# Another written-out order of all engine queues, with changed planner costs, in an attention and spectral-mixing kernel

## The chip, the cores and the metric

The kernel runs on one core of a Trainium2 chip. Five engines of the core work side by side, each on its own queue of instructions: TensorE (PE in the profile; its weight loads are listed apart as PEld) does matrix products from SBUF into PSUM, VectorE (DVE) and ScalarE (ACT) do elementwise work and can read PSUM, GpSimd (POOL) does elementwise work on SBUF, and SyncE (SP) issues most transfers between device memory and SBUF. The metric is the device time of one execution in microseconds, the median of several runs.

## The reference

Two branches read the same x, of 2048 rows and 640 columns in bf16; a gate mixes their outputs row by row.

```python
x = A_x
g = _sigmoid((x * gate_w).sum(-1, keepdims=True))
a = _A_ref(x, A_wq, A_wk, A_wv, A_wo, A_beta)
b = _B_ref(x, B_w_r, B_w_i)
return g * a + (1 - g) * b
```

Branch A projects x to q, k and v with 32 heads of 20 columns, and takes the rows in four segments of 512, one after another. In each segment it does causal softmax attention; from the second on it also reads a memory that the earlier segments left (a product of phi(k) and v, and the sum of phi(k), where phi(t) is t + 1 above zero and exp(t) below). Both are mixed by a gate for each head, and the result is projected with wo:

```python
p = _softmax(logits, axis=-1)
a_dot = jnp.einsum('bhqk,bhkd->bhqd', p, vs)
pq = phi(qs)
num = jnp.einsum('bhld,bhde->bhle', pq, M)
den = jnp.einsum('bhld,bhd->bhl', pq, z)[..., None] + 1e-06
a_mem = num / den
o = g * a_mem + (1.0 - g) * a_dot
```

Branch B transforms all of x by a two-dimensional real Fourier transform, multiplies it by a table of weights, and transforms it back:

```python
X = jnp.fft.rfft2(x.astype(jnp.float32), axes=(-2, -1))
W = w_r + 1j * w_i
X = X * W
y = jnp.fft.irfft2(X, s=(S, D), axes=(-2, -1)).astype(jnp.bfloat16)
```

(The last two blocks are cut and written without the wrapping functions.)

## The kernel before

The program is recorded first as a list of 2353 small operations, in the class `Kern`, and laid out and emitted afterwards by the class `Sched`. An operation names the engines that can do it, what it reads and writes, and a cost for each engine. Many evictions of PSUM have two engines to choose from (`copy_alts`: ScalarE or VectorE), and so have some additions from SBUF to SBUF (`either`: VectorE or GpSimd).

What sets the order is `ORDER` (L556), a tuple of 2353 numbers written into the kernel. Half of a number, rounded down, is the operation; its last bit picks the engine. For each engine the order of its instructions is that of the tuple. `schedule` (L109) walks through the queues with the costs, and from the times that it works out it places the PSUM banks (four for the attention logits, four for everything else, L552), the semaphores of transfers, and the point up to which earlier transfers must have landed before a new one is issued (`WINDOW`, 1,600,000 bytes in flight). Tile positions of TensorE, called modes in the code, also follow from the order: 0 for the full array, 1 for four rows of tiles (the logits), 2 for four columns of tiles. `emit` (L239) then writes the instructions with their waits. Since all matmul helpers issue at L496 (mode 2 pieces) and L498, all PSUM copies at L507 (ScalarE) and L509 (VectorE), and all transfers at L526 (transposed) and L528, the profile tells them apart by their tiles.

The work, with the names that the code gives it:

- *Loads* (`ld_...`, `xT`): x comes twice, once plain into `xsb` in eight pieces for branch B, and once transposed into `xT` for each segment; weights and tables follow. The first transposed piece feeds the first projections (`projd`). Sixteen dummy matmuls on a zeroed tile (`warm`) run before.
- *Branch A*: `proj` makes q and k, evicted (`ev_proj`) and stored (`st_q`, `st_k`), then loaded again with heads padded to 32 partitions (`pad_q`, `pad_k`). `vproj` makes v. The logits are 80 units `qk` of four PSUM banks each; ScalarE's exp (L1137) empties each unit into `ex`, GpSimd zeroes the part above the diagonal (`mask`, L1140), `pv` multiplies with v, and VectorE scales the result into `on` (L1167, L1170, L1172). phi is an exp on ScalarE (L1010) and a max and a min on VectorE (L1021, L1022). The memory is updated (`mupd`, `m_add`, `m_mask`) and read (`memrd`, L1078 to L1082), and added by `addmem` (L1177). `on` is stored (`st_o`), loaded transposed (`oT`) and projected with wo (`oproj`, L496).
- *Branch B*: `fold` (L860, L865) adds and subtracts halves of x, and matmuls named F1, D, T, Tb, Db and Fb apply the transforms from tables. Their evictions are `ev_F1`, `ev_D`, `ev_Tb`, `ev_Db`; `W_mul` (L1287) and `W_add` (L1292) multiply by the weights; `sum_Db` (L1333) leaves the result in `G`.
- *Gate*: a few four-column operations for each segment (L937 to L955, of which L947 and L948 cast the gate to two bf16 halves), a transposing matmul (`gateT`), a store, and a load that spreads it over partitions (`gbc`). `gate_tab` (L968) multiplies it into a table by which Fb brings branch B into the PSUM bank of the output; `oproj` adds branch A there, `final` evicts it, and `st_out` and `st_part` store it.

The softmax here doesn't subtract the row's maximum and nothing guards it: scores larger than these inputs give would overflow.

## Time and profile before

| what | value |
|---|---|
| median of 4 runs | 246.53 us (246.17 to 247.04) |
| the profiled execution | 247.91 us |
| its span, first to last instruction | 246.2 us |
| mean granted TensorE clock | 0.993 |
| busy: TensorE, weight loads | 231.8, 140.2 us |
| busy: VectorE, ScalarE, GpSimd | 198.7, 201.5, 132.1 us |
| moved by DMA | 36.71 MB |

A busy time is the union of an engine's instructions, in microseconds. Matmuls are pipelined, so a TensorE that shows as busy need not be at its peak. In a row of an instruction the order is: start, length, engine, line, operation, output and inputs, shapes, and in brackets the idle time of the engine ahead of it with what ended it. A chain is followed back from the last instruction, at each step to what released it; its shares are shares of the span.

### The profile page before, as it was taken

The page shows a single profiled execution, that of the slowest core. Times are in us where ns is not written, and L with a number is a line of the kernel's source. Part 1 is how long each engine was busy: PE and PEld are TensorE (multiplying, and loading weights), DVE is VectorE, ACT ScalarE, POOL GpSimd, SP SyncE. Part 2 cuts the span into 40 slices and gives each one's busy share as a digit, 9 for nine tenths or more (in the row PEclk, how much of TensorE's full clock was granted, in tenths as well). Part 3 has the DMA queues.
Part 4 walks back from the last instruction along what each step waited for, and adds up shares of the span by engine and source line. Part 5 has one row for each costly group of instructions (what it writes and reads, how often), then busy time and mean ns, then how long its engine had stood idle before and what let it go on. Part 6 is the DMA issues. An engine that isn't in the chain of part 4 may idle for free.

```text
span 246.2 us, 8884 instructions
## 1 busy us (share of the span) xinstructions
PE 231.8 (94%) x3681; PEld 140.2 (57%) x3702; DVE 198.7 (81%) x534; ACT 201.5 (82%) x204; POOL 132.1 (54%) x200
## 2 busy tenths in 40 slices
PE   7899999999899999999888999999899999999994
PEld 2344565556556557556543565655555657667683
DVE  1489997988999898889997999989999975643743
ACT  2088799999998999999874998888899878798820
POOL 8421861262557684464974385646567656407610
PEclk9999999999999999999997999999999999999999
DMA  7998966695695666766442546313353857685224
GB/s 183 331 360 220 215 172 173 198 203 136 149 176 111 173 123 143 234 183 200 107 99 53 143 115 186 97 59 104 111 111 68 213 148 79 81 124 112 79 67 125
DMA packets 55880, 36.71 MB, mean 149 GB/s; under 512 B 31792, under 2 KB 52128, under 8 KB 55840
## 3 DMA queue, kind: packets, MB, share of 16 engines
q1 hardware_dynamic: 54144, 35.32, 58.3%
q10 hardware_dynamic: 1696, 0.82, 1.1%
q8 instruction: 29, 0.48, 0.8%
q14 instruction: 11, 0.09, 0.1%
HBM read 19.86 MB, written 9.71 MB: 120 GB/s over the span
## 4 chain that ended last, share of the span: by engine, by line
PE 65%; DVE 21%; DMA 6%; issue 3%; ACT 2%; SPq 1%; POOL 0%; DVEq 0%
PE psum L498 57%; PE psum L496 8%; DVE Pt L1287 5%; DMA xT<-in_A_x_dram 2%; DMA oT<-o_scr 2%; DMA o_scr<-on 2%; DVE qu L509 2%; DVE Cp L509 2%; ACT ex L1137 1%; SPq L528 1%; DVE Yt L1292 1%; DVE va L1045 1%; DVE on L1172 1%; DVE Ac L509 1%; DVE phk L1022 1%
## 5 line engine op out<-in xcount | busy, mean ns | idle before, releaser
L1137 ACT ACTIVATE ex<-psum 128x2048 bf16<-128x2048 f32 x80 | 150.2, 1878 | 17.9 <-PE psum L498 16.7
L1140 POOL TENSOR_SCALAR_AFFINE_SELECT ex<-ex 128x512 bf16<-128x512 bf16 x128 | 81.0, 653 | 72.7 <-ACT ex L1137 68.7
L498 PEld LDWEIGHTS psum<-va,ex 128*128 128x128 bf16 x1280 | 39.0, 96 | 5.8 <-issue 1.3
L498 PE MATMUL psum<-va,ex 128*128 128x21 bf16 x1280 | 41.2, 173 | 0.3 <-issue 0.2
L498 PE MATMUL psum<-qp,kp 20*128 20x384 bf16 (+3 forms) x512 | 31.7, 301 | 1.3 <-ACT ex L1137 0.3
L498 PE MATMUL psum<-wv,xT 128*128 128x500 bf16 (+1 forms) x160 | 32.0, 301 | 0.4 <-issue 0.2
L498 PE MATMUL psum<-xT,wk 128*128 128x512 bf16 (+1 forms) x129 | 30.5, 386 | 1.5 <-DMA xT<-in_A_x_dram 1.0
L498 PE MATMUL psum<-xT,wq 128*128 128x512 bf16 (+1 forms) x125 | 29.9, 388 | 1.4 <-DVE Bt L509 1.2
L1287 DVE TENSOR_TENSOR Pt<-psum,Wt 128x642 bf16<-128x642 f32 x32 | 25.4, 822 | 0.8 <-PE psum L498 0.5
L496 PE MATMUL psum<-wo,oT 128*32 128x320 bf16 x480 | 23.2, 300 | 0.3 <-issue 0.3
L498 PEld LDWEIGHTS psum<-qp,kp 20*128 20x128 bf16 x512 | 9.1, 92 | 18.4 <-ACT ex L1137 9.9
L509 DVE CAST ot<-psum 128x320 bf16<-128x320 f32 x21 | 10.0, 490 | 11.7 <-PE psum L496 8.6
L498 PE MATMUL psum<-big,Ac 128*128 128x321 bf16 (+2 forms) x96 | 17.9, 257 | 1.2 <-DVE Cp L509 0.4
L498 PEld LDWEIGHTS psum<-wv,xT 128*128 128x128 bf16 x160 | 13.3, 97 | 10.0 <-DVE Ac L509 0.8
L1045 DVE TENSOR_TENSOR va<-psum,ebx 128x500 bf16<-128x500 f32 (+1 forms) x32 | 15.2, 484 | 3.6 <-PE psum L498 2.8
L498 PE MATMUL psum<-tt,Yt 128*128 128x256 bf16 (+1 forms) x96 | 17.3, 277 | 0.5 <-DVE qu L509 0.2
L509 DVE CAST qu<-psum 128x512 bf16<-128x512 f32 x20 | 13.7, 687 | 4.8 <-PE psum L498 4.8
L1292 POOL TENSOR_TENSOR Yt<-Pt 128x321 bf16<-128x321 bf16 x18 | 13.4, 756 | 7.2 <-DVE Pt L1287 4.7
L498 PEld LDWEIGHTS psum<-xT,wk 128*128 128x128 bf16 (+1 forms) x140 | 10.1, 98 | 11.8 <-issue 3.8
L1333 DVE TENSOR_TENSOR G<-eo,psum 128x320 bf16<-128x320 f32 x32 | 14.9, 480 | 1.7 <-PE psum L496 0.9
L1177 POOL TENSOR_TENSOR on<-on,mem 128x320 bf16<-128x320 bf16 x16 | 12.8, 807 | 5.8 <-DVE on L1172 5.8
L1172 DVE TENSOR_TENSOR on<-psum,rs 128x320 bf16<-128x320 f32 x32 | 15.3, 481 | 0.6
(85 smaller groups left out, 379.7 us busy)
## 6 DMA issues: line engine op xcount, KB each, us to landing
tt<-tab_tt SPq DMA_DIRECT2D x16, 256.0 KB, 3.3
xsb<-in_A_x_dram SPq DMA_DIRECT2D x8, 320.0 KB
kp<-k_scr SPq DMA_DIRECT2D x28, 80.0 KB
qp<-q_scr SPq DMA_DIRECT2D x28, 80.0 KB
o_scr<-on SPq DMA_DIRECT2D x12, 160.0 KB
out_dram<-ot SPq DMA_DIRECT2D x12, 160.0 KB
q_scr<-qu SPq DMA_DIRECT2D x6, 256.0 KB
k_scr<-qu SPq DMA_DIRECT2D x6, 256.0 KB, 3.3
```

Of the source, the lines that this page charges most:

```text
L496: h = e.matmul(dst, wt, r_, start=st, stop=sp_, **{**kw, "tile_position": (0, q), "skip_group_check": True})
L498: h = e.matmul(o_, l_, r_, start=st, stop=sp_, **kw)
L509: alts["dve"] = (lambda e: e.tensor_copy(dst(), src()), 67 + 1.04 * n, 68.0)
L528: return e.dma_start(d_, s_)
L1045: self.one("dve", lambda e: e.tensor_tensor(va.ap(i * H * VW + h0 * VW, [VW, nh], [1, DH]), self.ps(bank, 0, [DH, nh], [1, DH]), self.ebx. ...
L1137: self.one("act", lambda e: e.activation(dst(), src(), ACT.Exp, scale=SC), 4 * width, [bank], [self.exb(s, g, j) for g, j in outs], prio - ...
L1140: self.one("pool", lambda e, g=g, j=j: e.affine_select(self.ex.ap(self.exo(s, g) + JOFF[j], [1280, 4], [1, P]), self.ex.ap(self.exo(s, g) ...
L1172: self.one("dve", lambda e, rs=rs, bank=bank, g=g: e.tensor_tensor(on.ap(80 * g, [D, 4], [DH, 4], [1, DH]), self.ps(bank, 0, [88, 4], [VW, ...
L1177: self.either(lambda e, g=g: e.tensor_tensor(on.ap(80 * g, [D, 4], [1, 80]), on.ap(80 * g, [D, 4], [1, 80]), self.mem.ap(80 * g, [D, 4], [ ...
L1287: self.one("dve", lambda e, ri=ri, Pt=Pt, Wt=Wt, bank=bank: e.tensor_tensor(Pt.ap(ri * 322, [644, 2], [1, KD]), self.ps(bank, 0, [0, 2], [ ...
L1292: fn = lambda e, r=r, a0=a0, a1=a1, op=op, Pt=Pt, Yt=Yt: e.tensor_tensor(Yt.ap(r * 322, [1, KD]), Pt.ap(a0 * 322, [1, KD]), Pt.ap(a1 * 322 ...
L1333: self.one("dve", lambda e, q=q, n2=n2, bank=bank, eo=eo: e.tensor_tensor(self.G.ap(n2 * D + 639 * q, [1 - 2 * q, 320]), eo.ap(q, [1, 320] ...
```

## The change

The tuple `ORDER` is replaced as a whole. With it come changed costs for the planning pass: higher fixed costs for GpSimd, other times for four kinds of transfer, the limit on transfers in flight counted when the pass picks the next instruction (before, it was only turned into a wait), and the two gate casts, under the new name `gate_cast`, counted as instructions that VectorE and GpSimd cannot run at the same time (as is `gate_tab`). No operation of the computation is added or taken away. Lines behind the first edits stand ten or so further down in the changed kernel.

```diff
+        if name in ("gate_cast", "gate_tab", "den_gate") and not o.banks:
+            o.lock = True
...
+        def window():
+            tot, i = 0, len(issued) - 1
+            while i >= 0 and tot <= self.WINDOW:
+                tot += issued[i].nbytes
+                i -= 1
+            return issued[i] if i >= 0 else None
+
         def head(e):
...
+            if o.dma:
+                gate = window()
+                if gate is not None:
+                    t = max(t, gate.t1 + self.HOP)
             if e == "dve" and o.lock:
                 t = max(t, free["pool"])
...
-        fix0, per0, late = {"act": (65, 0.833, 110.0), "dve": (67, 1.04, 68.0), "pool": (100, 0.945, 50.0)}[eng]
+        fix0, per0, late = {"act": (65, 0.833, 110.0), "dve": (67, 1.04, 68.0), "pool": (132, 0.945, 50.0)}[eng]
...
-        return self.Sc.op({"dve": (fn, 67 + 0.52 * n, 68.0), "pool": (fn, 70 + 1.95 * n, 50.0)}, r=r, w=w, prio=prio, name=name, after=after, lock=True)
+        return self.Sc.op({"dve": (fn, 67 + 0.52 * n, 68.0), "pool": (fn, 120 + 1.95 * n, 50.0)}, r=r, w=w, prio=prio, name=name, after=after, lock=True)
...
-        "ld_fcat": (400.0, 350.0, 16), "ld_g": (400.0, 1050.0, 16), "ld_gc": (580.0, 200.0, 16), "ld_gw": (420.0, 600.0, 16),
+        "ld_fcat": (400.0, 350.0, 16), "ld_g": (400.0, 1500.0, 16), "ld_gc": (580.0, 200.0, 16), "ld_gw": (420.0, 600.0, 16),
...
-        "ld_wo": (600.0, 700.0, 16), "ld_wo2": (600.0, 3000.0, 16), "ld_wv": (450.0, 3000.0, 16), "ld_x": (450.0, 950.0, 16),
+        "ld_wo": (600.0, 3000.0, 16), "ld_wo2": (600.0, 3000.0, 16), "ld_wv": (450.0, 3000.0, 16), "ld_x": (450.0, 950.0, 16),
...
     ORDER = (
...
-        self.one("dve", lambda e: e.tensor_copy(hi(), sl(self.om)), 4, [b("om", s)], [b("hi", s)], prio + 3.0, name="gate_ops")
+        self.one("dve", lambda e: e.tensor_copy(hi(), sl(self.om)), 4, [b("om", s)], [b("hi", s)], prio + 3.0, name="gate_cast")
...
-                self.ex.ap(self.exo(s, g) + JOFF[j], [1280, 4], [1, P]), self.ex.ap(self.exo(s, g) + JOFF[j], [1280, 4], [1, P]),
-                [[0, 4], [1, P]], ALU.is_ge, 0.0, base=0, channel_multiplier=-1), 512, [], [self.exb(s, g, j)], prio, name="mask")
+                [[0, 4], [1, P]], ALU.is_ge, 0.0, base=0, channel_multiplier=-1), 512, [], [self.exb(s, g, j)], prio, fix=105, name="mask")
```

What the two tuples make of the queues, by name: TensorE has 3702 matmul pieces before and 3657 after (a full-array matmul in mode 2 is issued in up to four pieces of 32 columns, and 15 of the Db matmuls no longer are), and 175 changes of mode before, 171 after. On another engine than before are 104 instructions. In sums, VectorE gets three more folds, three more `addmem` and two more `ev_proj`, and gives up two `W_add` to GpSimd and six evictions of branch B and of the last transposes to ScalarE. On SP the first transposed load of x stands ahead of the first plain one; the load of wo, and the transposed loads of the third and fourth segment, stand later.

## The prediction

> **What bounds the kernel now.** I read the page's busy shares and slices first, then the chain that ended last, then the engines by stretch, and last single places of the timeline.
>
> The page:
>
> ```profile
> PE 231.8 (94%) x3681; PEld 140.2 (57%) x3702; DVE 198.7 (81%) x534; ACT 201.5 (82%) x204; POOL 132.1 (54%) x200
> PEclk9999999999999999999997999999999999999999
> PE 65%; DVE 21%; DMA 6%; issue 3%; ACT 2%; SPq 1%; POOL 0%; DVEq 0%
> ```
>
> TensorE (PE) holds two thirds of the chain, VectorE (DVE) a fifth. In the 40 slices of the span VectorE shows 7 to 9 tenths busy from the 3rd to the 33rd (about 200 us), and 3 to 7 after. One slice has a lowered TensorE clock.
>
> The engines by stretch (length; busy us and instructions of PE, PEld, DVE, ACT, POOL; clock; DMA):
>
> ```profile
> 90.00:120.00 30.00, 29.34 (x416) 18.28 (x417) 26.70 (x78) 28.15 (x29) 16.87 (x26) 1.00 0.64 171
> 120.00:135.00 15.00, 12.31 (x131) 6.11 (x131) 13.29 (x30) 10.51 (x12) 9.97 (x16) 0.89 0.36 87
> 165.00:195.00 30.00, 28.14 (x412) 16.75 (x418) 28.31 (x89) 26.99 (x24) 18.52 (x27) 1.00 0.45 112
> ```
>
> The stretch 120 to 135 is a hole: TensorE idles 2.69 us there, and the clock of 0.89 over 15 us means 0.11 x 15 = 1.7 us more lost. Together 4.4 us.
>
> The chain at the start and before that hole:
>
> ```profile
> 0.80 0.41 SPq L528
> 1.27 5.96 DMA xT<-in_A_x_dram
> 7.37 5.27 PE psum L498 x89
> ...
> 119.46 0.56 DVE gate L944
> 120.02 0.60 DVE qu L509
> 120.62 0.93 DVE Cp L509 x2
> 121.54 0.67 DVE omh L947
> ...
> 130.29 0.44 DVE Bt L509
> ```
>
> The first matmul waits for the transposed x, and that DMA stood behind another on SP's queue. From 114.6 to 130.8 the chain is nearly all VectorE, in which two four-element gate operations cost 0.56 and 0.67 us.
>
> The timeline and the instructions of one line:
>
> ```profile
> 187.85 1.88 ACT L1137 ACTIVATE ex<-psum 128x2048 bf16<-128x2048 f32 x1 [0.17 <-PE psum L498]
> 189.78 0.12 PEld L498 LDWEIGHTS psum<-qp,kp 20*128 20x128 bf16 x8 [0.29 <-ACT ex L1137]
> 190.23 1.88 ACT L1137 ACTIVATE ex<-psum 128x2048 bf16<-128x2048 f32 x1 [0.17 <-PE psum L498]
> ```
>
> ```profile
> 119.21 0.79 POOL L1177 TENSOR_TENSOR on<-on,mem 128x320 bf16<-128x320 bf16 x1
> 119.35 0.67 DVE L944 TENSOR_TENSOR gate<-gate,gate 128x4 f32<-128x4 f32 x1
> 120.65 1.54 POOL L1177 TENSOR_TENSOR on<-on,mem 128x320 bf16<-128x320 bf16 x2
> 121.47 0.74 DVE L947 CAST omh<-gate 128x4 bf16<-128x4 f32 x1
> ```
>
> ```profile
> L947 DVE CAST omh<-gate x4: 101/152/744, 39.0 to 175.9; 128x4 bf16<-128x4 f32 x4
> ```
>
> A logits unit cannot start before the exp of the unit ahead has ended: 2.38 us from exp to exp. And a VectorE operation started under a GpSimd (POOL) one took up to 0.74 us where alone it takes 0.10.
>
> **The change, part by part.** The instructions are the same but for 45 fewer matmul pieces; what changes is their order on all five queues, and the engine of 104 of them. I laid both orders on one axis, TensorE's own work from the first projection on, with start-to-start times of this trace (216 ns for 512 columns, 137 for 320, 25 for 21) and 0.11 us for a change of tile mode: the logits matmuls whose loads start at 187.40 give way at 187.73, 0.33 us later, and hold 0.22 us of columns. That makes 218.6 us before; TensorE needs 242.5 - 7.3 = 235.2 us for it, so 16.6 us are waits. For the new order it is 217.8 us.
>
> 1. *Start.* On SP the first x transpose now stands ahead of the first plain load (0.41 us and a 0.06 us gap), so it is issued 0.47 us sooner. Taken: -0.5. Ends: -1.3 (the plain load's transfer, about 0.9 us, no longer shares the DMA engines) and +0.6 (the wq columns, first used at 8.02 us, are late next).
> 2. *Mode changes and warm-up.* 171 mode changes for 175: -0.4. One warm-up matmul (0.39 us at 7.70) stood after the first real ones and now stands ahead of them: -0.3. Ends: -0.8 and 0 (they were inside waits).
> 3. *Short loops through PSUM.* From the end of a matmul group to the matmul that waits for its emptied bank, TensorE needs other work as long as the emptying: about 0.26 us of latency (start of exp 0.45 us after the loads, less 0.22 us of columns, plus 0.05 after it) and the instruction, so 2.14 us for an exp. Before, 22 of the exp loops are shorter, by 4.8 us in sum; now 23, by 3.9. Loops through other evictions: 26 short by 3.7 us; now 21 by 2.3. If all counts: -2.3. If VectorE's queue is what really delays the eviction: 0. Taken: half, -1.1, since 65% of the chain is TensorE and 21% VectorE, and short loops overlap.
> 4. *Attention output back in.* Page order: o is stored, loaded transposed (3.0 to 5.7 us to landing), then projected. The shortest distances from the work that releases the load to its projection were 4.0, 5.1, 5.3 us of TensorE work; now 5.9, 6.0, 6.7. TensorE's weight loads waited 0.6 us for these; beside it a wait of 0.57 us for VectorE at 192.05 sits on a distance of 0.5 us that is now 0.9. Taken: half of 1.2, -0.6. Ends: -1.2 and 0.
> 5. *VectorE and GpSimd in each other's way.* Means less the shortest, over the six VectorE groups that overlap with GpSimd (phi max and min, W_add, folds, add of mem, gate casts), give about 10 us lost. The new order was laid out with the gate casts counted as clashing and with longer GpSimd times. Of the loss 21% is on the chain: -2.2 at best. Worse end: three folds and three memory adds go to VectorE, two W_add leave it, four more that can clash at 0.6 us, 21%: +0.5. Taken: -0.5.
> 6. *Moved evictions.* By their rows VectorE's total stays (+2.6 for folds and adds, +1.4 for projections, -3.9 for W_add, F1, D and Tb evictions). ScalarE gets 2.1 us more (201.5 busy of 246.2). It hides in the 0.5 us between two exps; if not, +2.1. Taken: +0.4.
> 7. *Folds at the start.* The first x load is issued some 1.75 us later, and VectorE gets more folding in the first 8.75 us of TensorE work (1.48 of it for 1.05). It hides in VectorE's idle 3.4 us between 7.3 and 30 us, and the folds' first readers are 8.6 us of work away. Taken: 0; with the cover gone +1.3.
> 8. *SP's later loads.* wo goes out 41 us of work later, the third and fourth x transposes 9 and 14 later; each still has 16 us of work or more before its reader, against landings of 3 to 7 us. 0. The DMA queues each moved step passes are the ones of parts 1, 4 and 7.
>
> Sum: -0.5 - 0.7 - 1.1 - 0.6 - 0.5 + 0.4 = -3.0 us. The profiled execution took 247.91 us, span 246.2; the median of four is 246.53, 0.6% lower. Taken from the median: 243.5.
>
> On part 5 the Trainium skill has a rule (SBUF — State Buffer, Who interferes with whom): GpSimd shares a port pair with VectorE, whoever starts first holds it for the whole instruction and the other blocks, and any VectorE instruction with two SBUF inputs clashes with a GpSimd read. The 0.67 us at 119.35 agrees. The rule speaks against the change: that gate product has two SBUF inputs, and the new plan does not count it among the clashing ones. By the rule only the casts (0.6 us lost) are planned away; part 5 would be 21% of that, -0.1, and the sum -2.6.
>
> **Rivals.**
> *The hole closes.* VectorE's work per 8.75 us of TensorE work peaks at 1.40 and 1.39 (marks 105, 122) before, now 1.34 and 1.20. If its 4.4 us go, some 1.4 of which parts 3 and 5 may hold already: 243.5 - 3.0 = 240.5. Against it: summed up to mark 114 VectorE has 13 us more work than TensorE in both orders (instruction lengths, which overlap a little).
> *VectorE takes back the gain.* Its total is unchanged and it is busy 26.7 to 28.3 of 30 us up to 195 us. Then only parts 1 and 2 count, and part 6 eats them: 246.5.
> *A new hole (slower).* Before there is a lull at mark 79 (VectorE 0.96, ScalarE 0.84 of TensorE's work) between two crowded stretches; now that place has 1.17 and 1.18, after 1.14 and 1.24. If the backlog there reaches what it was at 114 to 130 us (16 us of VectorE in a row, 2.7 us idle in 15, the clock halved), a second hole costs 4.4: 243.5 + 4.4 = 247.9. Half that idle without the clock would leave it faster.
>
> **How the numbers follow.** Forecast 243.5 (241.8 to 245.7): 0.46. Hole closes: 0.16. VectorE takes it back, 246.5 within 1: 0.13, of which 0.04 faster, 0.06 the same, 0.03 slower. New hole: 0.25. A measurement here tells 0.3% (0.7 us) from nothing. Faster 0.66, same 0.06, slower 0.28. The range runs from just inside the closed hole, 240.8, to just beyond the new one, 248.3, which leaves about 0.2 out.
>
> **What would show it.** Right: first matmul near 6.9 us; weight loads wait for exps less than the 9.9 us of before; the L947 cast (10 lines further down after) never near 0.7 us; no wait of TensorE for oT; stretch 120 to 135 with under 2.7 us idle. Wrong: VectorE's share of the chain above 21%, a lowered clock in a second slice, the first folds or first exps later than before.

## The result, and the profile after

The new order is slower: median 248.52 us (246.13 to 251.76, 44 runs) against 246.82 us (245.63 to 253.78, 63 runs) of the old one on the same chips. The ratio of the two is 1.0044 with a 95% interval of 1.0029 to 1.0060, that is 0.4% or about 1.1 us slower. (The ratio leaves out runs that lie more than 1.5% above the quickest, which is why it is smaller than the quotient of the medians.) The prediction said 243.5 us, range 240.8 to 248.3.

The runs differ in one thing that the profiled one hides, the granted TensorE clock:

| | runs | mean span | mean clock | clock 0.997 or more |
|---|---|---|---|---|
| old order | 102 | 245.71 us | 0.9980 | 82 of 102 |
| new order | 44 | 246.88 us | 0.9888 | 2 of 44 |

(The old order's row is of all its runs beside the experiments below.) A stretch of 3.41 us at half clock costs about 1.7 us, half of it, and lowers the mean clock by 1.7 / 246 = 0.007. (Set side by side, the same pieces of the late stretch took 1.1 us longer at half clock in e11 below than in the quick run, and 1.8 us longer in e10 than in e18.) The difference of 0.0092 in the clock is then worth up to 0.0092 x 246 = 2.3 us, more than the 1.17 us by which the mean spans differ. So the lower clock is large enough to hold the whole loss. That the order would be the quicker one at full clock is not shown: its two runs there have spans of 244.4 and 246.8 us, the old order's 82 a mean of 244.9 (244.0 to 246.5).

The profiled execution of the new order took 246.13 us (span 244.4), the quickest of the 44 and one of the two at full clock; that of the old order, 247.91 us, had a lowered clock (0.993), as 20 of the 102 runs had. Read side by side, those two profiles show the difference with the wrong sign.

The page of the new order (busy times; its queue of instruction fetches; shares of the chain that ended last; the granted clock):

```profile
PE 229.0 (94%) x3636; PEld 140.1 (57%) x3657; DVE 195.8 (80%) x534; ACT 203.9 (83%) x208; POOL 125.7 (51%) x196
PEclk9999999999999999999999999999999999999998
q8 instruction: 29, 0.48, 0.8%
PE 66%; DVE 17%; ACT 5%; DMA 5%; issue 3%; SPq 2%; DVEq 0%
```

VectorE's share of the chain fell from 21% to 17%, ScalarE's rose from 2% to 5%, and no slice but the last has a lowered clock.

The engines by stretch (length; busy us and instructions of PE, PEld, DVE, ACT, POOL; clock; DMA):

```profile
90.00:120.00 30.00, 28.62 (x413) 17.75 (x415) 28.09 (x84) 28.50 (x30) 15.70 (x25) 1.00 0.54 153
120.00:135.00 15.00, 13.92 (x194) 8.45 (x194) 13.74 (x36) 14.24 (x15) 10.88 (x19) 1.00 0.50 113
165.00:195.00 30.00, 29.33 (x457) 17.38 (x456) 27.93 (x88) 27.51 (x27) 19.25 (x29) 1.00 0.43 112
215.00:235.00 20.00, 17.60 (x492) 12.80 (x484) 8.83 (x23) 13.21 (x13) 8.69 (x14) 1.00 0.59 97
```

The last of these stretches before:

```profile
215.00:235.00 20.00, 20.00 (x557) 13.80 (x547) 10.56 (x25) 16.82 (x16) 10.29 (x16) 1.00 0.52 99
```

The hole of 120 to 135 us went from 2.69 us of idle TensorE to 1.08, and 165 to 195 from 1.86 to 0.67. In exchange 90 to 120 lost 0.7 us, and 215 to 235, where the old order's profile shows TensorE busy all 20 us, now has 2.40 us idle.

The chain at the start, around 120 us and in that late stretch (start, length, what):

```profile
0.80 1.40 SPq L536
...
4.62 4.48 DMA xsb<-in_A_x_dram
...
120.22 3.92 DMA tt<-tab_tt
...
223.71 1.86 issue
```

The transposed x is issued first now. The plain x that the folds need came later (a link of 4.48 us). Near 120 us the chain runs through the landing of a table and no longer through the gate operations. At 223.71 TensorE waited for nothing that the profile can name.

The longest waits that bear on the prediction (engine and line, what for; total, times, longest):

```profile
PEld psum L508 <- ACT ex L1147: 12.1, 42, 0.6
DVE xf L870 <- DMA xsb<-in_A_x_dram: 6.8, 2, 6.0
PEld psum L508 <- DMA tt<-tab_tt: 0.9, 1, 0.9
PE psum L506 <- issue: 1.9, 1, 1.9
```

Before, the waits for the exps, for the plain x and for `oT` were:

```profile
PEld psum L498 <- ACT ex L1137: 9.9, 33, 0.5
DVE xf L860 <- DMA xsb<-in_A_x_dram: 3.6, 2, 2.9
PEld psum L496 <- DMA oT<-o_scr: 0.6, 2, 0.4
```

The weight loads wait longer for the exps (12.1 us for 9.9). No line of the new order's profile names `oT`, which had cost 0.6 us before.

One line by its source, the gate cast, and then TensorE's timeline around the stop (start, length, what, and in brackets the idle time ahead):

```profile
L957 DVE CAST omh<-gate x4: 106/162/647, 38.2 to 181.9; 128x4 bf16<-128x4 f32 x4
```

```profile
218.70 0.46 PE L508 MATMUL psum<-va,ex 128*128 128x21 bf16 x12
219.64 1.85 PE L508 MATMUL psum<-va,ex 128*128 128x21 bf16 x68 [0.48 <-issue]
221.43 0.40 PE L508 MATMUL psum<-qp,kp 20*128 20x256 bf16 x8
...
222.85 0.85 PE L506 MATMUL psum<-wo,oT 128*32 128x320 bf16 x20
225.57 0.59 PE L506 MATMUL psum<-wo,oT 128*32 128x320 bf16 x12 [1.86 <-issue]
```

One cast still takes 0.647 us instead of 0.106. In the timeline 80 short matmuls of P times V (21 columns each) run in a row at 219 to 221.5 us; the old order has such a row at 208 us. Then TensorE stops in the middle of the output projection of operation 2246, between two pieces of one accumulation, and the profile names no semaphore that it waits for.

### The profile page after: what moved, and what is told of

It reads as the page before. It is cut to its first block, busy times and chain, and to the rows that moved or that the text cites. A ratio compares the mean times of both kernels' runs of the same rounds, so it can differ in the third digit from the quotient of the medians.

```text
span 244.4 us, 8773 instructions
## 1 busy us (share of the span) xinstructions
PE 229.0 (94%) x3636; PEld 140.1 (57%) x3657; DVE 195.8 (80%) x534; ACT 203.9 (83%) x208; POOL 125.7 (51%) x196
## 4 chain that ended last, share of the span: by engine, by line
PE 66%; DVE 17%; ACT 5%; DMA 5%; issue 3%; SPq 2%; DVEq 0%
PE psum L508 58%; PE psum L506 8%; ACT ex L1147 5%; DVE Pt L1297 4%; DMA xsb<-in_A_x_dram 2%; DMA tt<-tab_tt 2%; DMA pkn<-phk 1%; SPq L536 1%; DVE va L1055 1%; DVE qu L519 1%; DVE Ac L519 1%; DVE phk L1031 1%; DVE phk L1032 1%; DVE Cp L519 1%; DVE Yt L1302 1%
## 5 line engine op out<-in xcount | busy, mean ns | idle before, releaser
L1150 POOL TENSOR_SCALAR_AFFINE_SELECT ex<-ex 128x512 bf16<-128x512 bf16 x128 | 79.8, 643 | 72.4 <-ACT ex L1147 67.7
L508 PE MATMUL psum<-va,ex 128*128 128x21 bf16 x1280 | 43.3, 173 | 1.2 <-issue 0.5
L508 PE MATMUL psum<-wv,xT 128*128 128x141 bf16 (+1 forms) x160 | 33.3, 301 | 0.9 <-DVE Pt L1297 0.5
L508 PE MATMUL psum<-xT,wk 128*128 128x512 bf16 (+1 forms) x130 | 29.4, 380 | 0.4 <-DVE rs L1177 0.2
L506 PE MATMUL psum<-wo,oT 128*32 128x320 bf16 x480 | 21.5, 300 | 1.9 <-issue 1.9
L508 PEld LDWEIGHTS psum<-qp,kp 20*128 20x128 bf16 x512 | 9.1, 92 | 18.9 <-ACT ex L1147 12.1
L1302 POOL TENSOR_TENSOR Yt<-Pt 128x321 bf16<-128x321 bf16 x20 | 14.8, 742 | 6.4 <-DVE Pt L1297 5.5
L508 PE MATMUL psum<-big,Ac 128*128 128x160 bf16 (+2 forms) x96 | 16.9, 257 | 0.7 <-DVE Cp L519 0.4
L519 DVE CAST qu<-psum 128x512 bf16<-128x512 f32 x22 | 14.9, 682 | 1.5 <-PE psum L508 1.3
L875 POOL TENSOR_TENSOR xsb<-xf 128x320 bf16<-128x320 bf16 (+2 forms) x8 | 6.6, 819 | 18.0 <-DVE xf L870 15.1
L506 PEld LDWEIGHTS psum<-wo,oT 128*32 128x32 bf16 x480 | 12.4, 97 | 5.9 <-issue 2.9
```

The lines of the kernel that those rows point to most:

```text
L506: h = e.matmul(dst, wt, r_, start=st, stop=sp_, **{**kw, "tile_position": (0, q), "skip_group_check": True})
L508: h = e.matmul(o_, l_, r_, start=st, stop=sp_, **kw)
L519: alts["dve"] = (lambda e: e.tensor_copy(dst(), src()), 67 + 1.04 * n, 68.0)
L875: self.either(lambda e, dst=dst, src=src, d0=d0, n=n, op=op: e.tensor_tensor(xs.ap(o + dst, [D, 2], [1, n]), xf.ap(src + d0, [321, 2], [1, ...
L1150: self.one("pool", lambda e, g=g, j=j: e.affine_select(self.ex.ap(self.exo(s, g) + JOFF[j], [1280, 4], [1, P]), self.ex.ap(self.exo(s, g) ...
L1302: fn = lambda e, r=r, a0=a0, a1=a1, op=op, Pt=Pt, Yt=Yt: e.tensor_tensor(Yt.ap(r * 322, [1, KD]), Pt.ap(a0 * 322, [1, KD]), Pt.ap(a1 * 322 ...
```

## The experiments

Two things were open: what lowers the clock, and whether the late stop or something earlier is behind it. "Full clock" is 0.997 or more. Ratios are against runs of the old order on the same chip.

| run | what it is | median us (runs) | ratio, 95% interval | full clock |
|---|---|---|---|---|
| e1 | new order again | 250.17 (6) | 1.0115 [1.0048, 1.0182] | 0 of 6 |
| e2 | old order, new planner costs | 247.05 (12) | 0.9989 [0.9956, 1.0021] | 12 of 12 |
| e3 | new head, old tail | 250.55 (12) | 1.0057 [1.0007, 1.0106] | 2 of 12 |
| e4 | old head, new tail | 251.66 (6) | 1.0172 [1.0106, 1.0238] | 3 of 6 |
| e5 | new, transpose later, table load earlier | 250.84 (6) | 1.0149 [1.0110, 1.0187] | 0 of 6 |
| e6 | new, late gate load earlier | 248.92 (6) | 1.0072 [1.0047, 1.0097] | 0 of 6 |
| e7 | e5 and e6 and one more | 256.41 (6) | 1.0413 [1.0373, 1.0453] | 0 of 6 |
| e8 | old, transpose later | 251.55 (6) | 1.0107 [1.0068, 1.0147] | 1 of 6 |
| e9 | new, transpose earlier | 252.79 (6) | 1.0231 [1.0178, 1.0284] | 0 of 6 |
| e10 | new, 48 pairs more at the start | 247.98 (12) | 1.0043 [1.0006, 1.0081] | 8 of 12 |
| e11 | new, gate load as early as in the old | 249.32 (6) | 1.0118 [1.0058, 1.0178] | 0 of 6 |
| e12 | e10 with the transpose later | 248.87 (12) | 1.0088 [1.0051, 1.0125] | 4 of 12 |
| e13 | new, 128 pairs more at the start | 248.95 (9) | 1.0082 [1.0055, 1.0109] | 0 of 9 |
| e14 | old, 48 pairs more at the start | 249.87 (6) | 1.0124 [1.0081, 1.0166] | 3 of 6 |
| e15 | new, transpose later | 247.85 (6) | 1.0069 [1.0047, 1.0091] | 0 of 6 |
| e16 | e3 with the transpose later | 249.73 (12) | 1.0011 [0.9961, 1.0061] | 4 of 12 |
| e17 | e16, joined 200 entries earlier | 248.93 (10) | 1.0079 [1.0042, 1.0116] | 3 of 10 |
| e18 | e10 again | 247.32 (8) | 1.0033 [0.9992, 1.0074] | 6 of 8 |

No version beats the old order.

### e1: the new order once more

No edit; a second trace of the same program, in a slower execution.

> The changed kernel once more. Theory T (the late stretch): the new order is some 1.8 us quicker than the old one while TensorE's clock is full, but leaves stretches late in the run, near 217 to 226 us, in which TensorE does so little that the clock is halved for 3.4 us, 1.7 us lost each time, in some executions and not in others: median near 248, executions with a clock of 0.997 or 0.993 near 246.5, those with 0.986 and less near 249.5; the trace shows a halved clock between 217 and 232 us unless the execution is one of the quick ones. Rival R (no gain anywhere): the order is as slow at any clock, and the first trace was a lucky one: executions at 0.993 are no quicker than the kernel before at 0.993.

Its span was 249.9 us, its clock 0.982. The granted clock was halved from 90.98 to 94.40 us and from 230.93 to 234.34. TensorE's timeline in front of both:

```profile
90.38 0.45 PE L508 MATMUL psum<-Bt,tt 128*128 128x321 bf16 x2 [1.71 <-DMA tt<-tab_tt]
...
229.00 0.59 PE L506 MATMUL psum<-wo,oT 128*32 128x320 bf16 x12 [2.14 <-issue]
```

The same run by stretch, cut on the 3.41 us grid of those clock changes:

```profile
87.57:90.98 3.41, 1.58 (x25) 0.92 (x26) 1.42 (x5) 2.82 (x3) 2.90 (x6) 1.00 1.23 150
90.98:94.40 3.42, 3.42 (x43) 1.75 (x41) 3.16 (x9) 2.02 (x3) 1.09 (x3) 0.50 0.88 217
...
227.50:230.93 3.43, 1.93 (x56) 1.41 (x55) 0.49 (x1) 0.96 (x1) 0.71 (x2) 1.00 0.45 112
230.93:234.34 3.41, 3.41 (x56) 1.65 (x56) 0.92 (x3) 2.09 (x3) 2.14 (x3) 0.50 0.03 4
```

In both places TensorE was busy 1.58 or 1.93 us of a cell of 3.41 us, and the next cell is at half clock. The Trainium skill (TensorE: Matmul & The Clock Gate, What's actually happening) says that the gate watches windows of 3413 ns that run freely, and that an idle one sends the clock to half. The trace agrees on the length (3.41 us between the changes here), but these cells were not idle.

TensorE's busy time is not what decides, though. Four cells of the late stretch, the first of the quick run (full clock behind it), the others of e11, e10 and e12 (half clock behind them):

```profile
222.53:225.95 3.42, 1.56 (x48) 0.99 (x40) 0.49 (x1) 1.23 (x1) 2.01 (x3) 1.00 0.56 126
223.07:226.49 3.42, 1.56 (x44) 0.90 (x36) 0.49 (x2) 0.97 (x1) 1.84 (x3) 1.00 0.27 66
219.72:223.14 3.42, 3.02 (x105) 2.58 (x101) 1.75 (x6) 3.33 (x4) 1.61 (x4) 1.00 0.90 96
220.24:223.66 3.42, 3.36 (x108) 2.72 (x105) 1.40 (x5) 3.33 (x5) 1.15 (x2) 1.00 0.87 95
```

An estimate from the shapes in the traces sorts the cells far better: count the columns that each matmul streams, times the part of the 128 x 128 array that it fills (0.16 for 20 x 128, 0.25 for 128 x 32), and set the sum of a cell against the 8,090 full-array columns that 512 in 216 ns make in 3.41 us. Of 1303 cells in the 20 traces (from 18 us to 4 us before the end), the 26 with half clock behind them have 0.15 to 0.37 of it, and only three others have as little; the four above have 0.40, 0.37, 0.31 and 0.37, in their order. No run was made to test this. By it a row of short or narrow matmuls counts as little work even while TensorE is busy, and where the grid of an execution happens to cut the work decides: the quick run has the late hole too (1.86 us), and no cell is halved.

The first hole has a cause by name: the table load of operation 628 landed after its reader.

### e2: the planner's costs alone

The changed kernel with the old tuple in place of the new one:

```diff
     ORDER = (
-        36, 0, 88, 38, 86,
+        36, 0, 86, 56, 38,
...
```

> The old order of all queues, with the changed costs of the planning pass: only the PSUM banks, semaphores and the points of transfers in flight that follow from the costs can differ. T and R: as the kernel before, 246.8 within 0.5. If the costs themselves do harm by the banks they pick: 247.5 or more.

No difference, and every one of 12 runs at full clock. The changed costs move PSUM banks and waits, and that costs and brings nothing that 12 runs show. The difference between the kernels is the tuple.

### e3 and e4: which end of the order

The first 2100 entries (up to about 211 us) of one order, then the rest in the order of the other, both with the new planner costs. At the join, e3 against the new tuple:

```diff
...
         4370, 4076, 4372,
-        4040, 4316, 4318, 4375,
+        3804, 4538, 3988, 1978,
...
```

and e4 against the old tuple:

```diff
...
         4402, 4542, 4184,
-        4360, 4546, 4544, 4074,
+        4545, 4362, 4364, 4366,
...
```

> The first 2100 of the 2353 entries as in the new order (up to 192 us of TensorE work, some 205 us of time), the rest in the relative order of the old one. T: the new order's gain without its late stretch: 245.0 to 245.8, clock 0.99 or more in nearly all executions. R: 247 to 248.5, as the changed kernel.

> The reverse: the first 2100 entries as in the old order, the rest in the relative order of the new one. T: the old order's time plus one or two halved windows late in the run: 248 to 249.5, clock 0.99 to 0.98. R: as the kernel before, 246.5 to 247.3.

e4 is slower, with a halved cell at 231.62 to 235.04 and TensorE's weight loads waiting 4.2 us for `oT` beside it. Its three runs at full clock still have spans of 248.6 to 250.4 us, so there it is not the clock alone. The new tail is bad also behind the old head. But e3 is slower as well, with 10 of 12 runs below full clock. Its one trace is of a run without a lowered clock (span 244.7) and shows neither the stop nor a halved cell, so what slowed the others isn't seen. The simple theory that all of the loss sits in the tail falls.

### e5, e8, e9: the 640 KB transpose in SP's queue

The new order issues the transposed x of segment 4 (operation 1744) at 85.8 us behind the table load 628 (84.1 us), the old one at 68.3 us. Numbers in the tuple are twice the operation, so they are 3488 and 1256 there; each diff shows a moved entry with its neighbours where it stood and where it went. e5, in the new tuple:

```diff
-        2478, 1276, 3488, 1278, 1281,
+        1322, 806, 3488, 3042, 1324,
-        1233, 2804, 1256, 2390, 1159,
+        790, 842, 1256, 1260, 3022,
```

> New order, with two entries of the transfer queue changed: the 640 KB transpose of x for segment 4, which the new order issues 1.3 us behind the table load of id 628, goes out behind 16 later entries (near 99 us, its first reader is near 124), and that table load goes out four entries earlier (near 81 us). Theory L (late landings): with the transpose off its back the load lands before its reader, the 1.71 us wait of the second transform for its table near 88 to 90 us is gone, and with it the halved window at 91 to 94; the late stretch is untouched, so a halved window near 231 to 234 still comes in part of the runs: 247.3 to 248.0 us against 248.5 for the new order. Rival D (diffuse: the new order loses by many small waits and evictions in each other's way, not by these landings): 248.2 to 248.8, and halved windows elsewhere before 100 us.

e8, in the old tuple:

```diff
-        1063, 732, 3488, 726, 734,
+        1190, 1256, 3488, 3024, 3026,
```

> Old order, with one entry moved: the 640 KB transpose of x for segment 4 goes from its place near 68.6 us to right behind the table load of id 628 (81.4 us), as in the new order. Theory L: the load lands later; its reader stands 6.0 us after the issue against 3.3 in the new order, so the wait is 0 to 1 us; if the pieces of the transform that follow stall too, a halved window near 90 us comes in part of the runs: 247.0 to 248.2. Rival D: no difference, 246.6 to 247.0.

e9, in the new tuple:

```diff
-        2478, 1276, 3488, 1278, 1281,
+        2764, 1160, 3488, 2766, 736,
```

> New order with one entry of the transfer queue moved: the 640 KB transpose of x for segment 4 goes out 18 entries earlier, right behind the table load of id 580 (near 71 us, two entries later than it stood in the old order), instead of behind the table load of id 628 (85 us). The table load stays where it is, so nothing is held behind it. Theory L (a transfer that lands late opens a hole in TensorE's work near 88 us, and the clock is halved behind it): 628 lands within 3 us of its issue, no wait of the second transform on its table above 0.5 us, no halved window between 86 and 97 us in the profile, granted clock of the timed runs 0.99 and above; the late stop stays: 246.0 to 247.5 us against 248.5. Rival D (the loss is diffuse): 248.0 to 249.0. Rival Q (each entry in the busy queue delays those behind it wherever it stands, as the runs with moved entries showed): a new wait on a spectrum weight or a packed key between 74 and 86 us, 249 to 252.

All three are slower, by more than the disputed effect, and each because the spectrum weights came late. In e8 SP's own timeline and VectorE's show it:

```profile
81.93 2.89 SPq L526 DMA_TRANSPOSE xT<-in_A_x_dram  x1
84.93 0.56 SPq L528 DMA_DIRECT2D Wt<-in_B_w_i_dram  x1
...
89.89 1.56 DVE L1287 TENSOR_TENSOR Pt<-psum,Wt 128x642 bf16<-128x642 f32 x2 [1.66 <-DMA Wt<-in_B_w_i_dram]
...
90.78 0.34 PE L498 MATMUL psum<-Mz,phq 128*128 128x154 bf16 x3 [1.39 <-DVE Pt L1287]
```

SP is held 2.89 us by issuing the transpose. The spectrum weights behind it go out 2.6 us later than in the old order (84.93 for 82.36), VectorE waits 1.66 us for them, TensorE 1.39 us for VectorE, and the clock is halved from 91.24 to 94.65. In e9 (transpose near 73 us) the same weights made VectorE wait 3.00 us at 82.06, with half clock from 82.23 to 89.06. In e5 it was the table load that held the queue: moved ahead, it waited on SP for its buffer until 84.50, and the weights stood behind it:

```profile
84.50 0.34 SPq L538 DMA_DIRECT2D tt<-tab_tt  x1
84.88 0.54 SPq L538 DMA_DIRECT2D Wt<-in_B_w_r_dram  x1
...
86.73 0.59 SPq L538 DMA_DIRECT2D Wt<-in_B_w_i_dram  x1
```

The last weight went out at 86.73 instead of 83.16, VectorE waited 2.21 us, TensorE 1.95, and two cells (89.93 to 96.76) were halved. So the edits did not test what they were made for. What they do show is that a transfer moved by a few entries in this queue opens a hole two steps further on, with half clock beside it in all three. (In e5 the clock fell at 89.93, before the hole of 1.95 us ended; the cell ahead, with 2.6 us of TensorE busy, has 0.34 by the estimate above.)

### e15: the transpose alone, later

```diff
-        2478, 1276, 3488, 1278, 1281,
+        1322, 806, 3488, 3042, 1324,
```

> New order with only the 640 KB transpose of x moved behind 16 later entries (near 101 us). Theory L: 628 lands within 3 us of its issue in the profile, no wait of the second transform on its table over 0.5 us, no halved window between 86 and 97 us; the stop at pair 3245 stays: 246.8 to 248.0. Rival D: 248.2 to 249.0 with a halved window near 90 us or a wait of over 1 us there all the same.

The theory's time came in (247.85, within 246.8 to 248.0), its reason did not. With the transpose gone from behind it, the table load 628 still took 4.05 us, where under 3 was expected, and its reader still waited:

```profile
88.30 0.45 PE L508 MATMUL psum<-Bt,tt 128*128 128x321 bf16 x2 [0.73 <-DMA tt<-tab_tt]
```

Over 12 traces with the new order's head that keep its place, this load of 256 KB landed after 2.6 to 3.1 us in nine, and after 4.05, 4.61 and 4.65 us in three (e15, e1, e13), with and without the transpose behind it. Its reader stands 3.3 us after the issue (84.13 to 87.45 in the quick run), in the old order 6.0 to 6.4 us. In those three it waited 0.73, 1.71 and 1.94 us, and the clock fell behind the two larger waits. So a late landing does not need the neighbour, and with the old lead none of the three would have made its reader wait. The edit did not remove the late landing, so e15's ratio (1.0069) does not say what this hole costs.

### e6, e7, e11: the late gate load

The new order issues the gate load of segment 4 (operation 2269) at 221.4 us, the old one at 200. e6 moves it (4538) and the gate store ahead of it (3804):

```diff
-        4066, 4476, 4538, 4068, 4096,
+        4038, 4506, 4538, 4370, 4076,
-        4512, 4514, 3804, 4297, 4516,
+        3972, 4246, 3804, 4280, 4188,
```

> New order, with two entries moved in the late stretch: the gate load of segment 4 (256 KB, issued at 221.4 us among the last attention transposes) goes out behind the transpose of id 2253 near 211 us, and the small gate store of segment 4 that it follows from 218.1 to before 198.8 us. Theory L: the stop of 1.9 to 2.4 us of TensorE at 223 to 226 us goes or falls under 1 us and no halved window follows at 230 to 235; the one at 91 to 94 stays in part of the runs: 245.5 to 247.5. Rival I (the stop is instruction supply at that place of the program, whatever the transfers): the stop stays within 0.3 us of 2, 248.0 to 248.8. Rival D: 248.2 to 248.8.

e7 is e5 and e6 together, and the table load 748 four entries earlier:

```diff
-        1399, 1394, 1496, 2670, 2668,
+        2624, 3100, 1496, 1500, 3102,
```

> Both moves together, and the table load of id 748 (which reaches its reader 4.0 us after its issue near 120) four entries earlier. Theory L: most runs at a granted clock of 0.995 or more, median 244.2 to 246.2 us, faster than both kernels. Rival I: 246.5 to 247.8. Rival D: 248.0 to 248.8.

e11 moves the two of e6 further:

```diff
-        4512, 4514, 3804, 4297, 4516,
-        4066, 4476, 4538, 4068, 4096,
+        4272, 1946, 3804, 4218, 4538, 4274, 4276,
```

> New order; the gate load of segment 4 and the small gate store ahead of it go out behind the attention transpose of id 2109 (near 195 us, where the old order has them near 200), far from the instruction fetches of 215 to 226 us; in the run before it only went to 211 us. Theory C (the fetch is late because the transfers of 215 to 223 us, this load among them, share its engines): the stop at pair 3245 shrinks to under 1 us and none comes at 3117: 246.5 to 248.0. Rival T (the stop comes from the pace, 128 pairs in 4.2 to 4.3 us against 4.7 in the old order, whatever this load does): the stop stays at 1.5 us or more, 248.0 to 249.0.

In e11 the stop is as long as ever (2.17 us at the same piece), so the gate load is not its cause. In e6 there were two stops:

```profile
221.21 1.95 PE L508 MATMUL psum<-va,ex 128*128 128x21 bf16 x68 [2.02 <-issue]
...
227.95 0.59 PE L506 MATMUL psum<-wo,oT 128*32 128x320 bf16 x12 [1.70 <-issue]
```

Counted in matmul-and-load pairs from the start of the program, the first is at 3117, the second at 3245: 128 apart. e7 is the worst of all, 4% slower; it has e5's late weights (a link of 3.26 us in the chain), both stops, and two cells at half clock behind each place. Delays did not hide each other: its excess of 9.6 us is more than those of e5 and e6 together (4.0 and 2.1). What its third edit does to that was not tried alone.

### e10, e13, e14, e18: is the stop instruction supply?

TensorE's instructions come in fetches of 16 KB: the page counts 29 packets and 0.48 MB for 3657 pairs, that is 126 pairs a packet. If the stop is a late fetch, it stands at one place of a grid of 128 pairs whatever work lies there. Splitting the dummy warm-up matmuls shifts the work against that grid and streams the same columns.

```diff
-            self.mms([(lambda k=k: (self.ps(bank, 0, [1, L]), t.ap(0, [1, P]), t.ap(P, [1, L]), True, True, {}), 1000)],
+            self.mms([(lambda k=k, j=j: (self.ps(bank, j * P, [1, P]), t.ap(0, [1, P]), t.ap(P + j * P, [1, P]), True, True, {}), 250) for j in range(4)],
```

e13 makes nine pieces of 56 columns of each; e14 is e10's edit in the old order; e18 is e10's program again.

> New order; each of the 16 warm-up matmuls of 512 columns is split into four of 128, which adds 48 matmul and weight-load pairs ahead of all the work and no streaming. Theory S (the stop of 2 us near 223 us is TensorE out of instructions: it came at pair 3245 of the program in all runs of the new order's tail, and in two at 3117 as well, 128 pairs or one 16 KB fetch earlier): every stop of over 0.6 us inside one operation stands at a pair of count 3245, 3117 or another that differs from them by a multiple of 128, which is 48 pairs earlier in the work, so not in the output projection of id 2246 at the same piece; time 247.5 to 249.5 us. Rival I2 (the stop belongs to that operation, a write or a bank): it stays at the same piece of id 2246, then pair 3293.

> New order; each warm-up matmul is split into nine of 56 columns, which adds 128 pairs, one whole 16 KB fetch, ahead of the work. Theory S: the fetch boundary falls on the same work as in the new order, so the stop of 1.5 to 2.5 us is back inside the output projection of id 2246, now pair 3373; 248 to 249.5 us. Rival W (the split warm-up itself removed the stop, by what it does to the start): no stop there, as with 48 more, 247 to 248.

> Old order with the same split warm-up (48 pairs more). Theory S: the old order has its 80 short matmuls of P times V in a row at 208 us and no stop to remove; a moved boundary may hit another place: within 1 us of 246.6, either side. Rival W (a split warm-up is worth 0.5 us or more by itself): 245.5 to 246.2.

> The kernel of e10 again, for a second trace. If this execution keeps the full clock throughout: theory B (what the stop took is given back before the end, at waits that stood behind it) has TensorE idle 1 to 2 us more than in the first trace at places after 195 us; theory E (other holes ahead of 195 us, from transfers that land late by chance) has the difference already at 195 us. Span 244.9 to 246.5 us, no stop of over 0.6 us inside an operation that is not at a pair of 45 over a multiple of 128.

The stops of over 0.6 us inside one operation, by pair:

| program | pair of the stop (us) | pair modulo 128 |
|---|---|---|
| new order, e1, e5, e9, e11, e15 | 3245 (2.17, 2.45, 2.35, 2.72, 2.17, 2.99) | 45 |
| e6, e7 | 3117 (2.13, 1.41) and 3245 (2.01, 3.26) | 45 |
| e10 and e12, 48 pairs shifted | none (0.37 and 0.43 at 3245) | 45 |
| e18, the program of e10 | 3373 (1.66) | 45 |
| old order with new costs, e2 | 3243 (0.85) | 43 |
| old order, e3, e4, e8, e14 | none | |
| e13, 128 pairs shifted | 3245 (1.13), and 0.54 at 3373 | 45 |
| e16 | none (1.10 at 3244 is a wait for `oT`) | |
| e17 | 2861 (1.98) | 45 |

(The times are from start to start of the two pieces.) With 48 pairs more, the stop left operation 2246 and came, in one of two executions, at the next boundary in other work; e18's timeline has it here:

```profile
226.54 0.31 PE L506 MATMUL psum<-wo,oT 128*32 128x320 bf16 x4
228.20 0.32 PE L506 MATMUL psum<-wo,oT 128*32 128x320 bf16 x4 [1.35 <-issue]
```

With 128 more, both boundaries fall on the work of before, and the stop is at the earlier of them (in the row of P times V), the later has 0.54 us where 1.5 to 2.5 was expected. e17, which has not the new tail, has a stop at the same place of the grid, 384 pairs earlier, and in the old order's profile and in e2 the weight loads pause for 0.71 us at 2861 too, which in e14 they do not. So the stop belongs to this grid and not to the work, which fits a TensorE out of instructions. Its packets do not show it as late: the last one recorded ahead of the stop had landed at 222.42 us in the quick run, 1.3 us before the stop, and at 220.90 in e13, 3.1 us before. That it is the pace of the short matmuls that runs it dry is argued: in the new order the 128 pairs ahead of the stop take 4.34 us (3.8 to 4.3 in the runs with the longest stops), in the old order's profile 4.74, and there it waits 0.03 us; but an old-order block of 4.10 us that ends at 211 us has only 0.28 us of idle time behind it, and the fetches of both orders are recorded with 0.9 to 1.5 us each. What makes TensorE stop at one boundary and not at the next was not found.

The shift brought 8 and 6 runs of 12 and 8 to full clock, against 2 of 44 (e12, with the same shift, 4 of 12). It did not bring the time below the old order, not even at full clock: the spans there have a mean of 246.2 us in e10 and 245.3 in e18, against 244.8 and 244.5 for the old order on the same chips. One thing that took the place of the stop is in all three traces of the shifted program (e10, e12, e18): TensorE's matmuls wait 1.2 to 1.3 us for `oT` near 210 us, which they do not in the quick run. e14 shows that the shift has a price of its own: the old order with 48 pairs more, an edit that does no work, is 1.2% slower (249.87 us, where 246.6 within 1 was expected). Its trace, of a run at full clock, has matmuls waiting 0.74 and 1.05 us for `oT`, which the old order's own trace does not have. The question that e18 was made for, where the time of the stop goes, stays open, since its execution had a stop.

### e12, e16, e17: both places at once

e12 has e10's edit of the warm-up and e15's of the tuple. e16 is e3 with e15's edit, so without the late stop and with the transpose away. e17 is e16 joined at entry 1900:

```diff
...
         3818, 1914, 1934,
-        3948, 1936, 1938, 3820,
+        3648, 3804, 4154, 3644,
...
```

> New order with the split warm-up (48 pairs more) and the 640 KB transpose of x for segment 4 moved behind 16 later entries of the queue (near 101 us; nothing else moved, so the table load and the spectrum weights keep their places). Theory L with S: the table load of id 628 lands within 3 us, no hole near 88 us, no stop near 223 us: 244.8 to 246.8 us, at or below the old order's 246.5. Rival D: as the split warm-up alone, 247.5 to 248.5. Rival Q (any other place of this transpose delays loads behind it): 249 or more, with a wait on a load issued after 100 us.

> The kernel of e3 (first 2100 entries of the new order, the rest in the old one's order, so without the run of 80 short matmuls at 219 us and without the stop) with the transpose of x for segment 4 moved behind 16 later entries as in e15. Theory L (the loss is the sum of the two holes): 244.5 to 246.3 us, below the old order. Rival M (an order away from the old one loses by halved windows somewhere else, so removing two of them does not bring it below): 246.8 to 250 us, with halved windows in most runs.

> As e16, with the join 200 entries earlier (first 1900 entries of the new order, near 190 us). Theory L: 244.5 to 246.5 us; the join may cost up to 1 us by transposes asked for in another order. Rival M: 246.8 to 250 us.

The rival held: no version falls below the old order. In e12's trace both places are clean (the table landed after 2.63 us, and there is no stop), and the clock is halved from 223.66 to 227.07 all the same. e16 shows what the order could do: its four runs at full clock have spans of 244.0, 244.2, 244.3 and 245.5 us, a mean of 244.5 against 245.2 for the 16 of the old order at full clock on that chip. Eight others were at 0.984 to 0.993 and took 247.5 to 250.0. In e17's trace the clock was halved from 116.81 to 123.64 and from 195.32 to 198.73, places where no other run has it.

Put together, the traces give one split. Between 200 us and the last work of TensorE a cell at half clock stands in 11 of the 13 traces of programs with the new tail (not in the quick run of the new order, nor in e18), and in none of the 7 without it (old order, e2, e3, e8, e14, e16, e17). The stop is not what the split goes by: three of the 11 have none (e4, e10, e12), and the quick run, e18 and e17 have one without a halved cell behind it. By the estimate in e1, the lowest cell between 200 and 236 us has 0.43 to 0.52 in the four traces of the old order (before, e2, e8, e14), and 0.15 to 0.37 in the 11.

## Why the prediction was wrong

The sum of the eight parts, -3.0 us, was made for a TensorE at full clock with instructions at hand. One of its terms was sized at nothing and one was left out, and the clock fell at both places.

*Where it failed.* Part 8, "SP's later loads", was taken at 0 because the loads that move far keep 16 us or more before their readers. It looked at those three loads and not at the ones with little to spare. In the tuples the lead of the table load 628 over its reader shrank from 6.0 us to 3.3, and e1, e13 and e15 show that it lands after up to 4.65 us: a wait of 0.7 to 1.9 us in three of twelve traces, and 1.7 us of half clock behind the longer ones. The second term was no part at all: the clock. The parts laid TensorE's work on one axis in start-to-start times at full clock, an axis that has no place for the supply of instructions, nor for how little of the array a stretch fills. In the late stretch, where the old profile shows nothing idle in 20 us, most traces of the new order's tail have now a stop of about 2 us, and 11 of 13, with the stop or without it, a halved cell. Over the runs the clock is 0.9888 for 0.9980. The distances in part 3 and 4 were also read against one duration each, though landings differ by 2 us from run to run.

*The size of it.* Per run the lower clock costs up to 2.3 us (0.0092 of 246) and the stop about 1.9; together 4.2. Taken from a predicted gain of 3.0 that would leave a loss of 1.2, against a measured one of 1.1 to 1.2. That the two sums meet proves no part of it: no run shows a gain of 3.0 (the quickest span of the new order's 44 is 244.4 us, of the old order's 102 it is 244.0), and where the stop was away and the clock full behind the new tail (e10, e12), the spans were longer than the old order's. So it is known what the sum left out; how much of the loss the clock, the stop and other waits each hold stays open.

*Part 1, start:* right. The first real matmul's load starts at 6.59 us in the quick run and 7.00 in e1 (7.34 before), -0.75 and -0.34 for -0.5.

*Part 2, mode changes:* cannot be told apart in these runs.

*Part 3, short loops through PSUM:* its sign test failed. The weight loads wait 12.1 us for exps, not less than 9.9. More waiting here stands beside less waiting elsewhere (the hole at 120 to 135 us has 1.08 us for 2.69), so part of a gain came, but not by this door. (The latency in the sum, 0.45 less 0.22 plus 0.05, is 0.28 us and not 0.26, which changes little.)

*Part 4, oT:* right in the profiled execution, where no wait of TensorE for `oT` is left. e1, the same program, has 0.5 us of weight loads waiting for it. In e4 and e14 matmuls wait 2.9 and 1.8 us, so it is a matter of the landing times again.

*Part 5, VectorE and GpSimd:* wrong in its sign test. A gate cast still takes 0.647 us. The gate product, by the rule of the Trainium skill that the prediction cited (SBUF — State Buffer, Who interferes with whom) the one left exposed, met nobody this time: 145 to 161 ns in all four. The 0.67 us of before agrees with the rule; when two such operations meet, it does not tell.

*Part 7, folds at the start:* the condition of the worse end, "the cover gone", came in, though these runs do not tell what it cost. VectorE waits 6.8 us for the plain x where it waited 3.6, its first fold starts at 7.23 us instead of 4.16, and a fold at 9.12 us sits on the chain behind a link of 4.48 us.

*The rivals.* "A new hole (slower)" was right in kind: a hole and a halved clock behind it, 247.9 us, one cell at 1.7. It was placed at mark 79 by the backlog of VectorE and ScalarE; the holes came from a transfer and from stops that no semaphore explains. Of the signs named for a wrong prediction, the first folds came later and e1 has a lowered clock in a second place; VectorE's share of the chain above 21% did not show (17%). So that this rival came nearest is partly luck. The range ended at 248.3; the median is 248.52.

*What misled.* The old profile was taken in an execution with a lowered clock, as 20 of 102 had, and the hole of 4.4 us at 120 to 135 looked like a property of the order. In e2, with the same tuple at full clock, TensorE idles 2.70 us there and the clock stays at 1.00: the hole is real, the 1.7 us of clock were chance.

## What to carry to other kernels

When an order has holes of 1 to 2 us, ask for every transfer how many microseconds lie between its issue and its reader, and set that against the slowest landing seen, not the median; here 3.3 us was too little in three of twelve traces, for landings of 2.6 to 4.65. A profile of one execution does not show how often the clock falls: read the granted clocks of all runs before weighing a hole. When the clock falls, look at how much of the array the cell ahead filled, and not only at whether TensorE was busy. And a written-out order can be good in ways that no sum of its parts shows: of 16 programs with another order or another number of instructions than the old kernel, none was faster, one could not be told from it (e16), and 15 were slower by 0.4% to 4%, one that only split dummy matmuls among them.

## What was unexpected of the hardware

- TensorE can stop in mid-operation for 0.9 to 3.3 us, on a grid of 128 matmul-and-load pairs (about one 16 KB packet of the instruction queue). The profile calls it "issue". A lack of instructions fits; that a packet landed late is not seen.
- The granted clock fell behind cells of 3.41 us in which TensorE was busy for 0.9 us (e15) and for 3.36 us (e12), and not behind one of 1.56 us (the quick run). The part of the array that the matmuls filled sorts these cells (0.16, 0.37 and 0.40, an estimate).
- Issuing one 640 KB transpose holds SP's queue for some 2.9 us (e8), and transfers behind it go out that much later. One 256 KB load of the same program landed after 2.7 us in the quick run and after 4.6 us in e1.
